# Second MLP: first products as two-by-two blocks with seven products, among the second products

## Chip, cores and metric

The kernel runs on one core of a Trainium2 chip. The metric is the device time of one execution in microseconds. The core has a TensorE (PE, matrix products into PSUM banks), a VectorE (DVE), a ScalarE (ACT), a GpSimd (POOL) and a SyncE (SP) that issues the DMAs between DRAM and SBUF. Each engine runs its own instructions in the order of the program; semaphores tie them together.

## The reference, cut to what matters

Attention with a learnt bias on 4 x 8 heads of 576 tokens gives x of 2304 tokens x 512, then two MLPs follow:

```
x = attn_out ...reshape(2304, 512)
h = x @ w_in           # first MLP: 512 x 2048
g = h - np.tanh(h)
x = g @ w_out          # 2048 x 512
h = x @ w_in           # second MLP, weights of its own
r = np.maximum(h, 0.0)
g = s * (r * r) + b
out = g @ w_out
```

All is float32. The kernel writes each operand as a sum of a rounded part ("hi") and a rest ("lo") in the fp32r format and forms three of the four cross products, so a product costs three matmuls.

## The kernel before, in words

The attention comes first (lines 207 to 555). During it, a part of the first MLP's weights and the first tokens are fetched and split.

Then one loop runs over `seq`, all (c, f): ten chunks c of tokens (five for each MLP: 512 tokens, one chunk of 256 in each) and 16 blocks f of 128 hidden units. Step n does for its (c, f) the **first product** `gemm1` (line 323: 12 matmuls of 128x128 weights by the chunk's columns into one of two PSUM banks `h`), the `gate` (ACT squashes, DVE combines; in the second MLP a DVE scale and shift follows) and, one step later, the `split` (ACT casts to hi, DVE subtracts to lo). Two steps later comes the **second product** `gemm2` (line 567): in the first MLP 12 matmuls with the weights standing, in the second MLP three for each 128 tokens, with the tokens standing and 512 output columns. It adds up over f in PSUM banks `a0` to `a3`, which leave over SBUF to DRAM (`x2_d`, or `out_x`) after the 16th f.

PE's order in a step is thus: first product of n, second product of n-2.

**Weights** arrive as raw 64-bit words (two 32-bit halves; 512 KB for 128x512 numbers). Decoding one is `begin` (POOL takes the sign, ACT scales), `high` and `low` (two DVE instructions), and `both` (ACT casts, POOL subtracts). `weights_tick` does one stage each of three pieces; the step decides by `want` how many are due. In the last chunk of the first MLP the loop fetches the second MLP's pieces (`fetch(16 + m)`, line 618), into the slots of the first, two per step. **Tokens** of the next chunk are loaded and split on the POOL in steps 5 to 14 of a chunk (`load_x`, lines 298 to 319).

All DMAs of the loop are issued by SP in the order of the program, save two of the very end (line 603). `ring` (line 295) is a pool of 11 SBUF tiles of 576 columns.

## Time and profile before

| | us |
|---|---|
| median of 3 runs | 1073.44 (1071.9 to 1073.63) |
| the profiled execution | 1073.4 |
| its span, first to last instruction | 1071.6 |
| PE busy | 1059.9 |
| DVE busy | 575.9 |
| ACT busy | 461.9 |
| POOL busy | 339.3 |

The attention ends at about us 273 of the span, the first MLP runs to about 680, the second to the end. Busy times are shares of the whole span. The granted TensorE clock of the profiled execution was 1.0 throughout. To read a row of a timeline: its start in us, its length in us, engine, line of the kernel, operation, tiles, shape and how many instructions are merged in it. A merged row of matmuls is longer than the distance to the next row, because the modelled end of one overlaps the next; the pace is the distance between starts.

### The profile page before, as it was taken

To read this page: it belongs to the slowest core of one execution; us is meant where nothing else is said; L and a number is where in the kernel's file an instruction comes from. 1 tells how busy PE (TensorE), PEld (TensorE's weight loads), DVE (VectorE), ACT (ScalarE), POOL (GpSimd) and SP (SyncE) were. 2 spreads that over 40 slices of the span, in tenths; PEclk is the share of its full clock that TensorE was granted. 3 is DMA by queue.
4 is the path that set the end of the run, shared out by engine and by line. 5 is a ranking of instruction groups with operands and counts; after the bars stand their busy time and mean duration, and the time that the engine had idled before them with its cause. 6 is when DMAs were issued, how large, how long until landed. Compare 5 with 4: busy or idle time off the path is not lost.

```text
span 1071.6 us, 18296 instructions
## 1 busy us (share of the span) xinstructions
PE 1059.9 (99%) x7000; PEld 836.5 (78%) x7000; DVE 575.9 (54%) x1159; ACT 461.9 (43%) x955; POOL 339.3 (32%) x518
## 2 busy tenths in 40 slices
...
GB/s 285 321 188 262 194 228 155 185 128 89 119 273 20 31 30 1 1 80 20 40 1 1 189 214 205 158 10 10 69 11 1 40 40 1 1 59 1 1 40 20
DMA packets 41335, 99.66 MB, mean 93 GB/s; under 512 B 5024, under 2 KB 11552, under 8 KB 41248
## 3 DMA queue, kind: packets, MB, share of 16 engines
...
q10 hardware_dynamic: 288, 0.26, 0.1%
...
## 4 chain that ended last, share of the span: by engine, by line
PE 90%; DVE 2%; POOL 1%; DMA 1%; issue 1%; ACT 0%; ACTq 0%; DVEq 0%; POOLq 0%
PE h L333 37%; PE a L587 37%; PE o L497 7%; PE s L398 6%; PE t L442 3%; POOL pn L436 1%; DMA qk<-in_qk 1%; PE c L442 1%; DVE raw L405 1%; ACT p L419 0%; DVE xo L504 0%; POOL w L89 0%; DVE pt L480 0%; DVE sm L427 0%; POOL sm L423 0%
## 5 line engine op out<-in xcount | busy, mean ns | idle before, releaser
L333 PE MATMUL h<-x,w 128*128 128x512 f32 (+1 forms) x1920 | 420.6, 368 | 0.0
L333 PEld LDWEIGHTS h<-x,w 128*128 128x128 f32 x1920 | 337.4, 188 | 62.4 <-issue 0.8
L342 DVE TENSOR_TENSOR h<-h,ring 128x512 f32<-128x512 f32 (+1 forms) x160 | 103.4, 646 | 348.2 <-ACT ring L341 348.1
L341 ACT ACTIVATE ring<-h 128x512 f32<-128x512 f32 (+1 forms) x160 | 88.8, 555 | 375.0 <-PE h L333 375.0
L587 PE MATMUL a<-ring,w 128*128 128x512 f32 (+1 forms) x960 | 210.2, 368 | 0.0
L587 PE MATMUL a<-w,ring 128*128 128x512 f32 x864 | 208.9, 389 | 0.0
L587 PEld LDWEIGHTS a<-ring,w 128*128 128x128 f32 x960 | 168.3, 189 | 30.0
L587 PEld LDWEIGHTS a<-w,ring 128*128 128x128 f32 x864 | 161.1, 188 | 32.7
L349 ACT CAST ring<-h 128x512 fp32r<-128x512 f32 (+1 forms) x160 | 87.1, 544 | 142.8 <-DVE h L344 108.0
L436 POOL TENSOR_SCALAR pn<-p,sm 128x576 f32<-128x576 f32 (+2 forms) x224 | 131.8, 605 | 41.5 <-DVE sm L427 37.1
L350 DVE TENSOR_TENSOR ring<-h,ring 128x512 fp32r<-128x512 f32 (+1 forms) x160 | 101.8, 636 | 74.0 <-ACT ring L349 69.2
L86 POOL TENSOR_SCALAR x<-xr 128x512 fp32r<-128x512 f32 (+1 forms) x36 | 20.6, 572 | 339.1 <-DMA xr<-x_d 339.1
L405 DVE CUSTOM_DVE_ANT_0 raw<-s,bias 128x576 f32<-128x576 f32 x144 | 103.8, 753 | 20.3 <-PE s L398 14.9
L419 ACT ACTIVATE p<-raw,mn 128x576 f32<-128x576 f32 x144 | 110.9, 774 | 7.7 <-DVE mn L405 4.3
L89 POOL TENSOR_TENSOR w<-wx,w 128x512 fp32r<-128x512 f32 x64 | 82.8, 1294 | 84.9 <-ACT w L148 82.8
L497 PE MATMUL o<-pt,vv 128*64 128x256 f32 (+1 forms) x640 | 95.0, 418 | 1.3 <-DVE xo L504 1.3
L398 PE MATMUL s<-qk 64*128 64x288 f32 (+1 forms) x640 | 91.7, 430 | 2.7 <-DVE mn L405 1.3
L398 PEld LDWEIGHTS s<-qk 64*128 64x128 f32 (+1 forms) x640 | 46.9, 175 | 43.9 <-DVE mn L405 18.3
L126 POOL TENSOR_SCALAR wsg<-w 128x512 f32<-128x512 f32 x64 | 41.8, 653 | 83.4 <-DMA w<-in_wts 82.8
L344 DVE TENSOR_SCALAR h<-h,sb_t 128x512 f32<-128x512 f32 (+1 forms) x80 | 61.2, 765 | 2.9
L442 PEld LDWEIGHTS t<-ident,pn 64*128 64x128 f32 x1184 | 51.8, 139 | 9.9 <-DVE pt L480 1.5
L497 PEld LDWEIGHTS o<-pt,vv 128*64 128x64 f32 x640 | 38.9, 136 | 24.1 <-DVE xo L504 1.7
...
## 6 DMA issues: line engine op xcount, KB each, us to landing
w<-in_wts SPq DMA_DIRECT2D x64, 512.0 KB, 4.9
...
```

What stands on the lines that cost most here:

```text
L333: nc.tensor.matmul(h, a, x, start=(k == 0), stop=(k == 3 * KD - 1))
L341: nc.scalar.activation(out=t, in_=h, func=(AF.Tanh, AF.Relu)[layer])
L342: nc.vector.tensor_tensor(out=h, in0=h, in1=t, op=(ALU.subtract, ALU.mult)[layer])
L349: nc.scalar.copy(gh, g)
L350: nc.vector.tensor_tensor(out=gl, in0=g, in1=gh.bitcast(F32), op=ALU.subtract)
L398: nc.tensor.matmul(o[0:n, c, 0:288], q[h, ee, t * 128:t * 128 + n], kk[h, ee], start=True, stop=True)
L405: nc.vector.tensor_tensor_reduce(out=raw.rearrange("p (c j) -> p c j", c=2), in0=s_t.pop((x, j))[:, :, 0:288], in1=bias_t[pairs[i][0], k]. ...
L419: nc.scalar.activation(out=p, in_=raw, func=AF.Exp, scale=-1.0, bias=mn, accum_out=sm[:, j:j + 1])
L436: nc.gpsimd.tensor_scalar(out=pn[:, c:c + b - a], in0=p[:, a:b], scalar1=sm[:, j:j + 1], scalar2=0.0, op0=ALU.mult, op1=ALU.add)
L442: nc.tensor.transpose(out_, in_, ident[ROWS[r], ROWS[r]])
L497: nc.tensor.matmul(o[h], v[:, e, j], unit_t[i, u][:, 8 if j == 4 else 4 * e + j, 0:n], start=(j == 0), stop=(j == 4))
L587: nc.tensor.matmul(o, x, y, start=first and j == 0, stop=last and j == 2)
```

## The change

The second MLP no longer runs in the loop over chunks. Its tokens are taken as three blocks of 768 (`SUPER`), each as two halves of 384 columns. For a pair p of hidden blocks (f = 2p and 2p+1) the first product is a two-by-two block product: two halves of the 512 input rows, two hidden blocks, two halves of tokens. It is formed with **seven products** in place of eight: sums of weight blocks times sums of token blocks, and sums of the results in PSUM (`X`, `Y`, `Z`, `V`, lines 833 to 874 of the changed kernel). A product is six matmuls of 384 columns. Two of the pair's four result blocks (first half of the tokens) go on at once, split into g1 and g2, and their second products stand among the next pair's products. The other two are held in SBUF and split later: after eight pairs, the second half's 16 second products run as one stretch, during which the next block's tokens are summed and split.

The second MLP's raw weights are fetched from step 18 of the first MLP on, one piece per step (`raw_next`, `keep`), decoded to float32 and stored to a DRAM tensor `w32_d`. The weights of a pair's first product are read back for each block (`load_w`), summed on the POOL (`combine`) and split on ACT and POOL (`part`). The second products' weights are read back once in the last chunk of the first MLP (`renew`, `renewed`). SBUF pools are arranged anew under one naming function (`place`); in the attention 11 raw loads of single pieces stand where 7 loads of two did.

**PE, second MLP.** Before, two groups of one step (h: first product, a: accumulators of the second; x tokens, w weights, ring the split units):

```order
L333 MATMUL h<-x_9918,w_8133 128x512 x6
L333 MATMUL h<-x_10059,w_8133 128x512 x6
L587 MATMUL a_10274<-w_8087,ring 128x512 x3
L587 MATMUL a_10278<-w_8087,ring 128x512 x3
L587 MATMUL a_10282<-w_8087,ring 128x512 x3
L587 MATMUL a_10286<-w_8087,ring 128x512 x3
```

After, one pair of the last block (XA, C: sums of tokens and of weights, split; a: accumulators of the first half's tokens):

```order
L828 MATMUL X<-XA,C_11015 128x384 x6
L828 MATMUL Y<-C_10725,C_11015 128x384 x6
L828 MATMUL Z<-C_10725,C_11015 128x384 x6
L828 MATMUL V<-XA,C_11015 128x384 x6
L582 MATMUL a_11043<-w_8071,ring 128x512 x3
L582 MATMUL a_11047<-w_8071,ring 128x512 x3
L582 MATMUL a_11051<-w_8071,ring 128x512 x3
L828 MATMUL X<-C_10725,C_11015 128x384 x3
L828 MATMUL X<-C_10806,C_11015 128x384 x3
L828 MATMUL Z<-C_10806,C_11015 128x384 x6
L828 MATMUL V<-C_10806,C_11015 128x384 x6
```

The first products moved from one bank of 512 columns to four banks of 384, with second products of the pair before between them; X, Z and V are each written twice.

**DVE, second MLP.** Before, two steps (multiply, scale and shift, subtract the cast):

```order
L342 TENSOR_TENSOR h_10671<-h_10671,ring_10684 128x512
L344 TENSOR_SCALAR h_10671<-h_10671,sb_t_82 128x512
L350 TENSOR_TENSOR ring_10689<-h_10671,ring_10688 128x512
L342 TENSOR_TENSOR h_10706<-h_10706,ring_10719 128x512
L344 TENSOR_SCALAR h_10706<-h_10706,sb_t_82 128x512
L350 TENSOR_TENSOR ring_10724<-h_10706,ring_10723 128x512
```

After, most of one pair (L844 to L846 sums of results, L734 and L727 multiply, L729 scale and shift, L741 subtract the cast):

```order
L844 TENSOR_TENSOR ring_11671<-Z_11667,ring_11670 128x384
L846 TENSOR_TENSOR Y_11666<-V_11668,ring_11671 128x384
L734 TENSOR_TENSOR Y_11666<-Y_11666,ring_11709 128x384
L727 TENSOR_TENSOR X_11665<-X_11665,ring_11720 128x384
L729 TENSOR_SCALAR X_11665<-X_11665,sb_t_77 128x384
L857 TENSOR_TENSOR Z_11667<-Z_11667,ring_11670 128x384
L741 TENSOR_TENSOR ring_11732<-X_11665,ring_11731 128x384
L727 TENSOR_TENSOR Z_11667<-Z_11667,ring_11735 128x384
L729 TENSOR_SCALAR Z_11667<-Z_11667,sb_t_77 128x384
L863 TENSOR_TENSOR V_11668<-V_11668,ring_11670 128x384
L741 TENSOR_TENSOR ring_11749<-Z_11667,ring_11748 128x384
L734 TENSOR_TENSOR V_11668<-V_11668,ring_11746 128x384
```

The three instructions of a step became thirteen of a pair, and those of X, Z and V follow one another on the four banks.

**SP, the 256-column chunk of the first MLP.** Before, the tokens of two next chunks and the stores of a finished chunk:

```order
L307 DMA xr<-x_d_72 128x256
L307 DMA xr<-x_d_73 128x256
L307 DMA xr<-x_d_74 128x256
L307 DMA xr<-x_d_75 128x256
L593 DMA x_d<-o 128x512 x4
L307 DMA xr<-x_d_72 128x512
L307 DMA xr<-x_d_73 128x512
```

After, the same stretch (st: raw pieces, w_d: the DRAM tensor of decoded weights, s: decoded pieces and tokens):

```order
L612 DMA w_d<-s_6572 128x512
L604 DMA st_6612<-in_wts 128x512
L612 DMA w_d<-s_6614 128x512
L588 DMA x_d<-ring 128x512 x4
L604 DMA st_6666<-in_wts 128x512
L612 DMA w_d<-s_6668 128x512
L604 DMA st_6712<-in_wts 128x512
L612 DMA w_d<-s_6714 128x512
L604 DMA st_6754<-in_wts 128x512
```

Between the token loads and the chunk's stores there now stand a raw load and a store of each step.

The diff, cut to its core:

```diff
-FT = {4 + 6 * F: F for F in range(7)}
+FT = {4 + 4 * k: k for k in range(11)}
...
-CHUNKS += [(1, i * 512, min(512, NT - i * 512)) for i in range(5)]
-NC1 = 5
-XF, XL, FF = 5, 3, 11
+SUPER = [(1, i) for i in range(3)]
+C1 = 18
...
+        def raw_next(j):
+            F, h = wq[j]
+            raw = place(f"st{j % 2}", [512], I64)
+            nc.sync.dma_start(out=raw, in_=wts[16 + F, h])
+            raw_w[32 + j] = words(raw)
+
+        def keep(j):
+            k = 32 + j
+            begin(k, raw_w.pop(k))
+            high(k)
+            low(k)
+            nc.sync.dma_start(out=w32_d[wq[j]], in_=wx_t.pop(k)[1])
...
+        def renew(f):
+            wx_t[f] = ring(F32)[:, 0:512]
+            nc.sync.dma_start(out=wx_t[f], in_=w32_d[f, 1])
+
+        def renewed(f):
+            x = wx_t.pop(f)
+            w = wt[f, 1] = weight(f, 1)
+            nc.scalar.copy(w[:, 0], x)
+            rest(w[:, 1], x, w[:, 0])
...
+        def load_w(q, p):
+            if p >= NF // 2:
+                q, p = q + 1, p - NF // 2
+            if q < len(SUPER):
+                wf_t[q, p] = place(f"st{p % 2}", [2, 512])
+                nc.sync.dma_start(out=wf_t[q, p], in_=w32_d[2 * p:2 * p + 2, 0].rearrange("f p n -> p f n"))
+
+        def combine(q, p):
...
+            w = wf_t[q, p]
+            a11, a12, a21, a22 = (w[:, j // 2, j % 2 * 256:j % 2 * 256 + 256] for j in range(4))
+            sums_ = sums_at[q, p] = place("XB", [4, 256])
+            s2, s3, s1, s4 = (sums_[:, j] for j in range(4))
+            for o, a, b, op in ((s1, a21, a22, ALU.add), (s2, s1, a11, ALU.subtract), (s3, a11, a21, ALU.subtract),
+                                (s4, a12, s2, ALU.subtract)):
+                nc.gpsimd.tensor_tensor(out=o, in0=a, in1=b, op=op)
+
+        def part(q, p):
+            w, sums_ = wf_t.pop((q, p)), sums_at.pop((q, p))
+            cs = cs_t[q, p] = place(f"C{(p + q) % 2}", [7, 2, 256], F32R)
...
+            for o, x in groups:
+                nc.scalar.copy(cs[:, o, 0], x)
+            for o, x in groups:
+                rest(cs[:, o, 1], x, cs[:, o, 0])
...
+            def put(u, i, x):
...
+                nc.scalar.copy(unit(u, i, 0), x)
+                nc.vector.tensor_tensor(out=unit(u, i, 1), in0=x, in1=unit(u, i, 0).bitcast(F32), op=ALU.subtract)
+
+            def minus(o, a, b):
+                nc.vector.tensor_tensor(out=o, in0=a, in1=b, op=ALU.subtract)
+
+            def first(i):
+                put(0, i, raw(i, 0))
+                minus(raw(i, 0), raw(i, 1), raw(i, 0))
+                put(3, i, raw(i, 0))
...
+            return [lambda: load(0, 2), lambda: load(1, 3)] + [lambda g=g, i=i: g(i) for g in (first, second, third, fourth, fifth, sixth)
+                                                              for i in range(2)]
...
+        def squashed(layer, c):
+            t = ring(F32)[:, 0:384]
+            nc.scalar.activation(out=t, in_=c, func=(AF.Tanh, AF.Relu)[layer])
+            return t
+
+        def now_units(layer, c, t):
+            nc.vector.tensor_tensor(out=c, in0=c, in1=t, op=(ALU.subtract, ALU.mult)[layer])
+            if layer:
+                nc.vector.tensor_scalar(out=c, in0=c, scalar1=sb_t[:, 0:1], scalar2=sb_t[:, 1:2], op0=ALU.mult, op1=ALU.add)
...
+        def later_units(layer, c, t, f):
+            g = held_unit(f)
+            if layer:
+                nc.vector.tensor_tensor(out=c, in0=c, in1=t, op=ALU.mult)
+                nc.scalar.activation(out=g, in_=c, func=AF.Identity, scale=sb_t[:, 0:1], bias=sb_t[:, 1:2])
...
+        def parted(x, gs):
+            nc.scalar.copy(gs[0], x)
+            nc.vector.tensor_tensor(out=gs[1], in0=x, in1=gs[0].bitcast(F32), op=ALU.subtract)
...
-            m = n - swap - LAG - 1
-            if 0 <= m < 16:
-                fetch(16 + m)
-            if FF + n < 16:
-                fetch(FF + n)
-            if m >= 1:
-                want = 32 + min(32, int(1.4 * m))
...
+            if C1 <= n < C1 + 32:
+                raw_next(n - C1)
+            if C1 < n <= C1 + 32:
+                keep(n - C1 - 1)
...
+            e = n - (NS - NF)
+            if e == 2:
+                load_w(0, 0)
+                load_w(0, 1)
+            if e == 6:
+                combine(0, 0)
+                part(0, 0)
+                combine(0, 1)
+            for _ in range({8: 2, 10: 1, 11: 1, 12: 2, 13: 2, 14: 2, 15: 1}.get(e, 0)):
+                xq.pop(0)()
+            if SUPER[0][0] and e >= LAG:
+                if e - LAG >= 1:
+                    renewed(e - LAG - 1)
+                renew(e - LAG)
...
+        fill = [lambda: gemm2(*seq[-2]), lambda: gemm2(*seq[-1])]
+        for q, (layer, s_) in enumerate(SUPER):
...
+            def product(o, p, a, u, begins):
+                cs = cs_t[q, p]
+                for i in range(2):
+                    for j, (l, r) in enumerate(((0, 0), (0, 1), (1, 0))):
+                        nc.tensor.matmul(o, cs[:, a, l, i * 128:i * 128 + 128], unit(u, i, r),
+                                         start=begins and i == 0 and j == 0, stop=i == 1 and j == 2,
+                                         skip_group_check=not begins)
+
+            pend = []
+            for p in range(NF // 2):
+                X, Y, Z, V = (bank(t) for t in "XYZV")
+                load_w(q, p + 2)
+                m1, u2, r = (ring(F32)[:, 0:384] for _ in range(3))
+                product(X, p, 4, 0, True)
+                nc.scalar.copy(m1, X)
+                if p + 1 < NF // 2:
+                    part(q, p + 1)
+                product(Y, p, 0, 1, True)
+                nc.vector.tensor_tensor(out=u2, in0=Y, in1=m1, op=ALU.add)
+                product(Z, p, 1, 2, True)
+                nc.vector.tensor_tensor(out=r, in0=Z, in1=u2, op=ALU.add)
+                product(V, p, 2, 3, True)
+                nc.vector.tensor_tensor(out=Y, in0=V, in1=r, op=ALU.add)
+                if pend:
+                    second_products(0, 2 * p - 2, pend.pop(0))
+                elif fill:
+                    fill.pop(0)()
+                t = squashed(layer, Y)
+                later_units(layer, Y, t, 2 * p + 1)
+                product(X, p, 5, 4, False)
+                t = squashed(layer, X)
+                now_units(layer, X, t)
+                product(Z, p, 6, 5, False)
+                nc.vector.tensor_tensor(out=Z, in0=Z, in1=u2, op=ALU.add)
+                g1 = two()
+                parted(X, g1)
+                t = squashed(layer, Z)
+                now_units(layer, Z, t)
+                product(V, p, 3, 6, False)
+                nc.vector.tensor_tensor(out=V, in0=V, in1=u2, op=ALU.add)
+                t = squashed(layer, V)
+                g2 = two()
+                parted(Z, g2)
+                later_units(layer, V, t, 2 * p)
+                if pend:
+                    second_products(0, 2 * p - 1, pend.pop(0))
+                elif fill:
+                    fill.pop(0)()
+                pend = [g1, g2]
+                if p + 1 < NF // 2:
+                    combine(q, p + 2)
...
+            xq = [] if final else tokens(q + 1)
+            for _ in range(2):
+                if xq:
+                    xq.pop(0)()
+            gs = {}
+
+            def ahead(f):
+                gs[f] = two()
+                parted(held_unit(f), gs[f])
+
+            ahead(0)
+            second_products(0, NF - 2, pend.pop(0))
+            ahead(1)
+            second_products(0, NF - 1, pend.pop(0))
+            if not final:
+                part(q + 1, 0)
+                combine(q + 1, 1)
+            for f in range(NF):
+                if f + 2 < NF:
+                    ahead(f + 2)
+                if f >= 2 and xq:
+                    xq.pop(0)()
+                if f >= 0:
+                    second_products(1, f, gs.pop(f))
+            while xq:
+                xq.pop(0)()
```

## Rows read from the trace of the kernel before

**Rows 1.** Page, part 1: engine, busy us (share of the span), instructions.

```profile
PE 1059.9 (99%) x7000; PEld 836.5 (78%) x7000; DVE 575.9 (54%) x1159; ACT 461.9 (43%) x955; POOL 339.3 (32%) x518
```

**Rows 2.** Timeline of PE in us 495 to 513: start, length, engine, line, operation, tiles, count.

```profile
495.95 1.60 PE L587 MATMUL a<-ring,w 128*128 128x256 f32 x12
497.39 2.91 PE L333 MATMUL h<-x,w 128*128 128x512 f32 x12
500.14 1.60 PE L587 MATMUL a<-ring,w 128*128 128x256 f32 x12
501.57 2.91 PE L333 MATMUL h<-x,w 128*128 128x512 f32 x12
...
508.50 2.88 PE L587 MATMUL a<-ring,w 128*128 128x512 f32 x12
511.22 2.88 PE L333 MATMUL h<-x,w 128*128 128x512 f32 x12
```

**Rows 3.** Groups by shape, whole span: line, engine, operation, shapes, count | busy us, mean ns | idle before.

```profile
L333 PEld LDWEIGHTS h<-x,w 128*128 128x128 f32 x1920 | 337.4, 188 | 62.4 <-issue 0.8 <-DVE ring L350 0.5
...
L342 DVE TENSOR_TENSOR h<-h,ring 128x512 f32<-128x512 f32 x128 | 89.5, 700 | 308.1 <-ACT ring L341 308.0
...
L89 POOL TENSOR_TENSOR w<-wx,w 128x512 fp32r<-128x512 f32 x64 | 82.8, 1294 | 84.9 <-ACT w L148 82.8 <-DVE sm L427 1.5 <-DMA w<-in_wts 0.3
...
L341 ACT ACTIVATE ring<-h 128x512 f32<-128x512 f32 x128 | 76.5, 598 | 330.7 <-PE h L333 330.7
L349 ACT CAST ring<-h 128x512 fp32r<-128x512 f32 x128 | 75.2, 587 | 118.2 <-DVE h L344 90.9 <-DVE h L342 27.3
...
L344 DVE TENSOR_SCALAR h<-h,sb_t 128x512 f32<-128x512 f32 x64 | 52.4, 819 | 2.3
...
L342 DVE TENSOR_TENSOR h<-h,ring 128x256 f32<-128x256 f32 x32 | 13.8, 432 | 40.1 <-ACT ring L341 40.1
...
L341 ACT ACTIVATE ring<-h 128x256 f32<-128x256 f32 x32 | 12.3, 384 | 44.4 <-PE h L333 44.4
...
L344 DVE TENSOR_SCALAR h<-h,sb_t 128x256 f32<-128x256 f32 x16 | 8.8, 551 | 0.6
...
L89 POOL TENSOR_TENSOR x<-xr,x 128x256 fp32r<-128x256 f32 x8 | 5.9, 738 | 0.7
```

**Rows 4.** Timeline of all engines over one step of the second MLP.

```profile
960.02 2.88 PE L587 MATMUL a<-w,ring 128*128 128x512 f32 x12
...
960.22 0.60 ACT L341 ACTIVATE ring<-h 128x512 f32<-128x512 f32 x1 [2.58 <-PE h L333]
960.85 0.70 DVE L342 TENSOR_TENSOR h<-h,ring 128x512 f32<-128x512 f32 x1 [2.49 <-ACT ring L341]
961.58 0.82 DVE L344 TENSOR_SCALAR h<-h,sb_t 128x512 f32<-128x512 f32 x1
962.49 0.58 ACT L349 CAST ring<-h 128x512 fp32r<-128x512 f32 x1 [1.68 <-DVE h L344]
```

**Rows 5.** Timeline of ACT and DVE in us 625 to 631.

```profile
625.70 0.62 ACT L148 CAST w<-wx 128x512 fp32r<-128x512 f32 x1 [0.61 <-DVE wx L140]
...
626.22 0.63 ACT L127 ACTIVATE y<-w 128x512 f32<-128x512 f32 x1
...
629.01 0.70 DVE L342 TENSOR_TENSOR h<-h,ring 128x512 f32<-128x512 f32 x1 [1.49 <-ACT ring L341]
...
629.61 0.69 DVE L133 SCALAR_TENSOR_TENSOR y<-y,wsg 128x512 int32<-128x512 int32 x1
```

**Rows 6.** SP's timeline at 642.8, then DMA issues of two stretches: count, KB, median us to landing.

```profile
642.82 0.42 SPq L113 DMA_DIRECT2D w<-in_wts  x1
...
w<-in_wts SPq DMA_DIRECT2D x1, 512.0 KB, 3.5
...
w<-in_wts SPq DMA_DIRECT2D x21, 512.0 KB, 4.3
```

**Rows 7.** Instructions of line 133 in the attention: ns min/median/max, first and last start.

```profile
L133 DVE SCALAR_TENSOR_TENSOR wx<-wx,wsg x8: 670/678/1790, 93.8 to 255.2; 128x512 int32<-128x512 int32 x8
```

281 lines of the change are left out of this document (178 added, 103 removed).

## The prediction

> **What bounds the kernel now.** I read the page's busy times first: the TensorE (PE) is busy for 99% of the span, the DVE (VectorE) for 54%, the ACT (ScalarE) for 43%, the POOL (GpSimd) for 32% [rows 1]. The PE is the bound, so any product that is saved is worth its full pace, as long as nothing new makes the PE wait. Next the timeline of the PE: in both MLPs groups of twelve products follow one another without a gap. A group of 512 columns starts 2.72 us before the next one, a group of 256 columns 1.44 us; where the two sizes alternate, a couple takes 2.75 + 1.43 = 4.18 us in place of 4.16 [rows 2]. So one product takes 226.7 ns at 512 columns and 120 ns at 256: 32 columns' worth beyond its own columns at 2.4 columns per ns, and 173.3 ns at 384 (an estimate on the line through the two rows).
>
> Then the work beside it: the groups by shape give the durations of the vector work at 512 and 256 columns, from which I take 384 halfway [rows 3]: relu 0.49 us (ACT), product or sum of a PSUM tile and an SBUF tile 0.57 (DVE), scale and shift 0.69 (DVE), cast 0.48 (ACT), and the subtraction of the cast like the product, 0.56 (DVE). One step's timeline gives the joints: a product's result is taken up 0.20 us after the next group starts, ACT to DVE and a DVE instruction that needs the one before cost 0.03, DVE to ACT 0.09 [rows 4]. Instructions of one engine that don't need each other overlap by 0.10 [rows 5].
>
> **The first products of the second MLP.** Before: four chunks of 16 groups at 2.72 and one of 16 at 1.44, 174.1 + 23.0 = 197.1 us [rows 2]. After: 3 blocks of 768 tokens x 8 pairs x 7 products x 6 matmuls = 1008 matmuls of 384 columns, 174.7 us. **Saved: 22.4 us.** The second products stay as they are (864 matmuls of 512 columns). The 384- and 512-column groups now alternate some 45 times at 0.02 each: **+0.9**.
>
> **The wait inside a pair.** A pair's PE work is X, Y, Z, V (4.16 us), nine second products (2.04), X, Z, V again (3.12), nine more (2.04): 11.36 us. Four PSUM banks serve it, so pair p+1 can't start Z before the split of Z of pair p has read it, nor V before the scale and shift of V has. I follow the chain from the end of X's last product (0): relu X 0.20 to 0.69, multiply 1.29, scale and shift 2.00, Z + u2 1.91 to 2.48 (overlapped), cast X 2.09 to 2.57, subtraction 3.17, relu Z to 3.06, multiply 3.10 to 3.66, scale and shift 4.38, V + u2 to 4.86, relu V 4.95 to 5.44, cast Z to 5.82, subtraction 6.42; then multiply V 6.89, scale and shift on the ACT 7.46. The PE, without waits, wants Z again at 2.08 + 2.04 + 2.08 = 6.20 and V at 7.24. With 0.1 for taking up a release it waits some 0.3 for each, of which V's wait holds Z's: 0.37 us per pair. It is the same in the next pair, since the DVE and the ACT then wait for X again. It bites from pair 1 to pair 7, six times a block, 18 times: **+6.7**. Bounds: 0 (chain 0.4 shorter) and 16 (0.9 each, 0.04 more on each of 15 instructions).
>
> **Pair 0 of the second and third block** has no second products to put between. The V sum ends at 4.93, relu and multiply of Y at 6.11, the ACT's scale and shift of Y at 6.68, and relu X, behind it on the ACT, starts at 6.58, 1.18 us later than its data. So X is free only at 9.55 where the PE wants it at 7.28 (2.4 lost), and Z at 12.80 where it then wants it at 11.73 (1.2): 3.55 each, **+7.1** for two; bounds 5 and 9. In the first block's pair 0 the last two steps of the first MLP fill the gaps with 2.72 each: nothing.
>
> **Raw weights beside the first MLP.** From step 18 on, each step loads one raw piece (512 KB), decodes it (ACT 0.63, DVE twice 0.69 [rows 5]) and stores it. In steps of 5.44 us this has room. In the 256-column chunk a step has 2.88 us. There are two staging tiles, so the load for step n+2 goes out after the decode of n and after its store on SP: 0.06 + 0.42 for the issue [rows 6], then the landing, 0.06, then 0.63 + 0.04 + 0.69 + 0.04 + 0.69. Two steps thus take 2.63 us + landing, and 5.76 are there: it closes at 3.1 us. In the trace such a load, 512 KB at the head of a burst, lands in 3.5 us; the median of its stage, where two or three go out together, is 4.3 [rows 6]. I take 3.8, since one store of half the size is ahead of it: 0.67 late per two steps. The ACT runs the decode ahead of the tanh of the step, so the lateness goes into the tanh, the split, and the two h banks; the PE feels it after about 2.2 us (3.5 us from the decode's start to the bank's release, against 5.76). The load of step 34 also stands behind the four stores of the finished chunk, which wait for the last accumulator's copy: about 2.7 late at once. 2.7 + 5 x 0.67 - 2.2 = **+3.9**; bounds 0 (landing 3.1) and 7 (landing 4.3).
> What the Trainium skill says here, page "DMA: Bandwidth & Descriptors", section "Anatomy of one DMA": about 2.0 us fixed plus the bytes at 436 GB/s, fitted on another path than SP's; that gives an estimate of 3.2 us, no trace row shows less than 3.5, and by it this term would be under 1 us.
>
> **Second halves.** While the PE runs 16 x 2.04 us of second products, the DVE subtracts held units from their casts, both operands in SBUF. In the first 7 us the POOL splits the next block's first weights. Of 8 DVE instructions with two SBUF operands in the attention, most took 0.67 us and the longest 1.79 [rows 7]: it stood behind a POOL instruction. The longest POOL instruction here has 1024 elements, 2.4 us (1.29 at 512, 0.74 at 256 [rows 3]). The subtraction for the third f is due 1.3 us after its cast. I take 0.5 in each of two blocks, **+1.0**; bounds 0 and 4.8.
>
> **At nothing.** Per pair the DVE has 13 instructions (7.6 us), the ACT 12 (6.4 with the weight parts), the POOL four sums and three splits (7.4), all under 11.36; their order is what costs, above. The weight loads (512 KB per pair) are issued a pair ahead. The 16 reloads of second weights stand a step ahead of their use in steps of 5.44 us; without that cover the ACT would wait in order, ahead of the split, some 2 us. The token sums have 12 steps of 2.04. In the attention 11 loads stand where 14 did: nothing, within 1 us. The tail has one more pair of stores, issued while products still run.
>
> **Sum** against the profiled execution (1073.4 us; span 1071.6, 1.8 around it; the median of the three runs is 1073.44, the same): -22.4 + 0.9 + 6.7 + 7.1 + 3.9 + 1.0 = -2.8, so 1070.6 us. A measurement of this kernel can tell about 0.2%, 2.1 us: it is a gain that is hardly larger.
>
> **Rivals.** *The chains close.* If the raw loads land in 3.1 us or the steps before them leave more room, and the pair's chain is 0.4 shorter, only pair 0 remains: -22.4 + 0.9 + 7.1 = -14.4, 1059.0; with one of the two open up to 1066. For it: DMA engines and vector engines are far from busy on the mean. Against: no row shows 3.1.
> *The pair's chain is longer* (the one that ends slower). Place: the split of Z, which ends the DVE's part of each pair. If each of its 15 instructions takes 0.04 more than halfway between the rows, a pair waits 0.97 and 18 of them 17.5: 1081.4. It is slower than before from 0.53 us per pair on. For it: four banks without a spare, and two engines in strict turns. Against: the same instructions kept 0.70 and 0.69 also while other engines were busy [rows 5].
> *The POOL holds the second halves.* Each of two blocks loses 2.4 us at its third f, +4.8 in place of 1.0: 1074.4. It holds if a subtraction waits for the whole POOL instruction, as the 1.79 us hint [rows 7]. The Trainium skill, page "SBUF — State Buffer", section "Who interferes with whom", says so: a DVE instruction with two SBUF inputs and a GpSimd one that reads SBUF exclude each other for the whole instruction. By that rule the pair's own chain is free, as each of its instructions has one PSUM operand.
> *The saving isn't there.* If 384 columns were paced by the weight load (188 ns [rows 3]), 1008 matmuls would take 14.8 us more: 1085.4. Against: 256 columns run at 120 ns [rows 2].
>
> **How the numbers follow.** Forecast 0.41 (1066 to 1076; about half of it, 0.22, under 1071.3, 0.16 within 0.2%, 0.03 above 1075.6). Chains close 0.25. Longer chain 0.24. POOL 0.08, within 0.2%. Weight pace 0.02. Faster 0.22 + 0.25 = 0.47; same 0.16 + 0.08 = 0.24; slower 0.03 + 0.24 + 0.02 = 0.29. The range 1059 to 1081 holds the forecast, the POOL case, most of the closing chains and half of the longer chain: a little over 0.8.
>
> **What would show it.** Groups of six 384-column products 1.04 us apart; PE waits on the DVE and ACT of some 0.4 us before Z and V in 18 pairs, and of 2.4 and 1.2 us at the second pair of the last two blocks; in the 256-column chunk ACT waits on raw loads and PE waits on the h banks that grow from the middle of the chunk; waits at the third f of a second half. Wrong it is if the PE waits elsewhere, above all at the start of the first block (a unit or a weight part that is late), or if the landings differ from 3.8 us.

## The result, and the profile after

The changed kernel takes **1082.1 us** (median of 4 runs, 1082.07 to 1082.66) where the kernel before took 1073.0 beside it: a ratio of **1.0087**, 95% interval 1.007 to 1.0105. It is slower by 0.9%, 9 us. The forecast was 1070.6 with a range of 1059 to 1081, so the time lies above the range and on the other side of no change.

The page's busy times, part 1 (engine, busy us, share of the span, instructions), under the span; to be read against [rows 1]:

```profile
span 1080.3 us, 19163 instructions
...
PE 1056.2 (98%) x7048; PEld 841.4 (78%) x7048; DVE 652.5 (60%) x1345; ACT 557.0 (52%) x1158; POOL 460.6 (43%) x630
```

PE's busy time fell by only 3.7 us, though 22.4 us of products went (in the last kernel below, which has the same products, it is 1040.3): a part of PE's lateness stands in its busy time. So I take the stages apart by the starts of groups on PE. PE's timeline, of before and then of after, where the first MLP begins and where the second one does (start, length, line, tiles, count):

```profile
273.70 3.02 PE L333 MATMUL h<-x,w 128*128 128x512 f32 x12
...
668.98 2.88 PE L333 MATMUL h<-x,w 128*128 128x512 f32 x12
```

```profile
272.56 3.02 PE L340 MATMUL h<-X,C 128*128 128x512 f32 x12
...
674.35 1.23 PE L828 MATMUL X<-XA,C 128*128 128x384 f32 x6
```

The attention ends 1.1 us earlier, yet the second MLP begins 5.4 us later: the first MLP lost **6.5 us**. From its first product to the end of the span the second MLP takes 406.0 us (1080.3 - 674.35) where it took 402.6: **3.3 more**, with 22.4 us of products saved. Both stages of the forecast came out worse.

Two pairs of the last blocks, on PE. The first fence is pair 5 of the second block, where everything is in its steady state; the second is the change from pair 0 to pair 1, also of the second block (in brackets: idle before, and who ended it):

```profile
870.42 1.23 PE L828 MATMUL X<-XA,C 128*128 128x384 f32 x6
871.49 1.21 PE L828 MATMUL Y<-C,C 128*128 128x384 f32 x6
872.64 1.34 PE L828 MATMUL Z<-C,C 128*128 128x384 f32 x6
873.82 1.32 PE L828 MATMUL V<-XA,C 128*128 128x384 f32 x6
874.99 2.25 PE L582 MATMUL a<-w,ring 128*128 128x512 f32 x9
877.08 1.23 PE L828 MATMUL X<-C,C 128*128 128x384 f32 x6
878.14 1.20 PE L828 MATMUL Z<-C,C 128*128 128x384 f32 x6
...
882.30 1.23 PE L828 MATMUL X<-XA,C 128*128 128x384 f32 x6
```

```profile
812.30 1.23 PE L828 MATMUL X<-XA,C 128*128 128x384 f32 x6
...
821.94 1.33 PE L828 MATMUL X<-XA,C 128*128 128x384 f32 x6 [2.17 <-DVE ring L741]
...
825.10 1.32 PE L828 MATMUL Z<-C,C 128*128 128x384 f32 x6 [0.78 <-DVE ring L741]
...
834.74 1.23 PE L828 MATMUL X<-XA,C 128*128 128x384 f32 x6
```

A steady pair takes 11.88 us (882.30 - 870.42). Groups that wait for nothing stand 1.04 to 1.07 apart, as forecast from [rows 2]; Z comes 1.15 after Y and V 1.18 after Z, and the second products 1.17 after V. A pair without any wait takes 11.49 (it is seen below); so a steady pair waits 0.38. Pairs 0 and 1 of the second block take 22.44 together, where 7.30 and 11.49 would do: 3.65 of waits.

The stages of all kernels that were run. "Start" is the first product of the second MLP; "pairs 1 to 3" are of the first block; "0 + 1" are the first two pairs of the second and of the third block; "pair 7 + half" reaches from the start of pair 7 to the next block's start, of the first and of the second block. All but "start" are differences of group starts on PE, in us; the ratio is to the kernel before, run beside it each time (medians from 1072.1 to 1073.0).

| kernel | start | steady pair | pairs 1 to 3 | 0 + 1 | pair 7 + half | span | median | ratio (95%) |
|---|---|---|---|---|---|---|---|---|
| before | 668.98 | | | | | 1071.6 | 1073.0 | 1 |
| after | 674.35 | 11.87 | 38.14 | 22.44, 22.46 | 51.26, 51.21 | 1080.3 | 1082.1 | 1.0087 (1.007 to 1.0105) |
| e_raw | 666.83 | 11.87 | 38.13 | 22.44, 22.44 | 51.21, 51.20 | 1073.0 | 1075.6 | 1.0029 (1.0018 to 1.0039) |
| e_noload | 667.60 | 11.88 | 38.13 | 22.44, 22.46 | 51.24, 51.24 | 1073.7 | 1075.8 | 1.0036 (1.0023 to 1.0049) |
| e_renew | 674.87 | 11.86 | 35.43 | 22.46, 22.44 | 51.21, 51.23 | 1078.2 | 1080.3 | 1.0071 (1.0056 to 1.0086) |
| e_swap | 674.81 | 11.49 | 35.66 | 22.71, 21.68 | 50.64, 50.64 | 1071.6 | 1074.0 | 1.0013 (1.0003 to 1.0023) |
| e_toks | 674.23 | 11.88 | 37.98 | 22.76, 23.11 | 49.35, 49.38 | 1077.3 | 1079.1 | 1.0060 (1.0045 to 1.0075) |
| e_fill | 674.38 | 11.88 | 38.14 | 23.38, 23.35 | 47.15, 47.13 | 1074.3 | 1075.7 | 1.0033 (1.0020 to 1.0046) |
| c_four | 667.19 | 11.49 | 34.48 | 21.66, 22.77 | 48.72, 48.76 | 1059.0 | 1062.1 | 0.9902 (0.9888 to 0.9917) |
| c_lock | 668.10 | 11.49 | 34.48 | 21.67, 22.81 | 48.21, 48.21 | 1058.8 | 1060.3 | 0.9888 (0.9872 to 0.9905) |
| c_fill | 668.44 | 11.49 | 34.48 | 22.99, 22.99 | 44.13, 44.13 | 1052.3 | 1053.8 | 0.9824 (0.9811 to 0.9838) |
| e_wait | 675.41 | 11.88 | 38.13 | 25.72, 25.75 | 51.24, 51.27 | 1088.0 | 1089.1 | 1.0157 (1.0139 to 1.0176) |

Read the row "after" against the ideal: three slow pairs in the first block (38.14, where three steady ones are 35.6), 3.65 us twice in "0 + 1", and a second half of 51.2 where 48.21 is possible. Four places, then, and the first MLP's 256-column chunk ahead of them. The experiments take them one by one.

### The profile page after: what moved, and what is told of

Same layout as the page of the kernel before. It is cut to its first block, busy times and chain, and to the rows that moved or that the text cites. A ratio compares the mean times of both kernels' runs of the same rounds, so it can differ in the third digit from the quotient of the medians.

```text
span 1080.3 us, 19163 instructions
## 1 busy us (share of the span) xinstructions
PE 1056.2 (98%) x7048; PEld 841.4 (78%) x7048; DVE 652.5 (60%) x1345; ACT 557.0 (52%) x1158; POOL 460.6 (43%) x630
## 4 chain that ended last, share of the span: by engine, by line
PE 77%; DVE 6%; POOL 4%; issue 3%; ACT 3%; DMA 2%; SPq 0%; ACTq 0%; POOLq 0%; DVEq 0%
PE a L582 25%; PE h L340 17%; PE o L504 7%; PE s L405 6%; PE Z L828 4%; PE V L828 4%; PE X L828 4%; PE t L449 3%; PE Z L582 3%; PE V L582 2%; DMA st<-in_wts 2%; PE Y L828 2%; POOL C L92 1%; POOL pn L443 1%; DVE ring L741 1%
## 5 line engine op out<-in xcount | busy, mean ns | idle before, releaser
L582 PE MATMUL a<-w,ring 128*128 128x512 f32 x576 | 147.0, 392 | 0.0
L349 DVE TENSOR_TENSOR h<-h,ring 128x512 f32<-128x512 f32 (+1 forms) x80 | 51.6, 645 | 143.8 <-ACT ring L348 143.7
L348 ACT ACTIVATE ring<-h 128x512 f32<-128x512 f32 (+1 forms) x80 | 44.2, 553 | 165.5 <-PE h L340 165.5
L582 PEld LDWEIGHTS a<-w,ring 128*128 128x128 f32 x576 | 107.6, 188 | 20.8
L340 PE MATMUL h<-X,C 128*128 128x512 f32 (+1 forms) x576 | 119.2, 356 | 3.9 <-DVE ring L357 3.8
L92 POOL TENSOR_TENSOR C<-st,C 128x512 fp32r<-128x512 f32 (+1 forms) x48 | 48.0, 1023 | 166.5 <-ACT C L652 166.5
L412 DVE CUSTOM_DVE_ANT_0 raw<-s,bias 128x576 f32<-128x576 f32 x144 | 103.9, 753 | 19.6 <-PE s L405 14.0
L340 PEld LDWEIGHTS h<-X,C 128*128 128x128 f32 x576 | 96.0, 189 | 22.0 <-DVE ring L357 6.2
L357 DVE TENSOR_TENSOR ring<-h,ring 128x512 fp32r<-128x512 f32 (+1 forms) x80 | 50.9, 637 | 38.2 <-ACT ring L356 38.2
L340 PE MATMUL h<-XA,C 128*128 128x512 f32 x288 | 70.7, 390 | 0.0
L828 PE MATMUL Z<-C,C 128*128 128x384 f32 x288 | 60.3, 344 | 3.0 <-DVE ring L741 3.0
L340 PEld LDWEIGHTS h<-XA,C 128*128 128x128 f32 x288 | 53.8, 188 | 11.3 <-issue 0.2
```

Source lines behind the costliest of these rows:

```text
L92: nc.gpsimd.tensor_tensor(out=lo, in0=raw, in1=hi.bitcast(F32), op=ALU.subtract)
L340: nc.tensor.matmul(h, a, x, start=(k == 0), stop=(k == 3 * KD - 1))
L348: nc.scalar.activation(out=t, in_=h, func=(AF.Tanh, AF.Relu)[layer])
L349: nc.vector.tensor_tensor(out=h, in0=h, in1=t, op=(ALU.subtract, ALU.mult)[layer])
L357: nc.vector.tensor_tensor(out=gl, in0=g, in1=gh.bitcast(F32), op=ALU.subtract)
L412: nc.vector.tensor_tensor_reduce(out=raw.rearrange("p (c j) -> p c j", c=2), in0=s_t.pop((x, j))[:, :, 0:288], in1=bias_t[pairs[i][0], k]. ...
```

## Experiment 1: raw pieces out of the 256-column chunk

```diff
+        RAW_AT = [*range(18, 32), *range(48, 66)]
-            if C1 <= n < C1 + 32:
-                raw_next(n - C1)
-            if C1 < n <= C1 + 32:
-                keep(n - C1 - 1)
+            if n in RAW_AT:
+                raw_next(RAW_AT.index(n))
+            if n - 1 in RAW_AT:
+                keep(RAW_AT.index(n - 1))
```

> The changed kernel, but no raw weight piece is loaded, decoded or stored in the 256-column chunk of the first MLP: pieces 0 to 13 stay at steps 18 to 31, the other 18 move to steps 48 to 65. In the changed kernel the first product of the second MLP starts at us 674.35 of the span, 5.4 later than before although the attention ended 1.1 earlier. Theory (the loads and decodes don't fit into steps of 2.88 us): some 6.5 us come back, the first product of the second MLP starts at about 667.9, total about 1075.6. Rival (a step of 5.44 us next to the last chunk's token loads is full as well, the lateness only moves): it starts between 672 and 674, total 1080 to 1082.

Measured: start 666.83, 7.5 us earlier than in the changed kernel, total 1075.6. Of the 7.5, 1.0 stands ahead of the first MLP, which starts at 271.56 in place of 272.56; the first MLP itself takes 395.27, as before (395.28), in place of 401.79. All later stages are the same to 0.1 us, so the 6.5 us are back: the loss was in this chunk, and steps of 5.44 us have room for the same work.

## Experiment 2: the decodes without the loads

```diff
-            raw = place(f"st{j % 2}", [512], I64)
-            nc.sync.dma_start(out=raw, in_=wts[16 + F, h])
-            raw_w[32 + j] = words(raw)
+            if not 14 <= j < 30:
+                staged[j % 2] = place(f"st{j % 2}", [512], I64)
+                nc.sync.dma_start(out=staged[j % 2], in_=wts[16 + F, h])
+            raw_w[32 + j] = words(staged[j % 2])
```

> The changed kernel without the 16 raw loads of the 256-column chunk: the pieces of steps 32 to 47 are decoded and stored as ever, but from the two staging tiles as they were filled before, so these weights are wrong and the time is read alone. Theory (a load's landing of 3.7 us in a loop of two staging tiles sets these steps): the steps take 2.9 us, the first product of the second MLP starts at about 668 in place of 674.35, total about 1075.6. Rival (the ACT and the DVE in turns set them: cast 0.37, scale 0.66, two decoding steps 1.39, the gate's subtraction 0.42 and the joints are 3.0 us without any landing): of 6.5 us at least 1.5 stay if it is that alone, nearly all if the DVE's place in the order is what counts; 670 to 674, total 1077 to 1082.

Measured: start 667.60, total 1075.8; so without the raw loads nothing of the loss is left, and decode and gate fit. The ACT's timeline of one step here (L137: decode; L348: gate):

```profile
484.40 0.66 ACT L137 ACTIVATE y<-st 128x512 f32<-128x512 f32 x1
...
486.13 0.38 ACT L348 ACTIVATE ring<-h 128x256 f32<-128x256 f32 x1 [1.07 <-PE h L340]
...
487.28 0.66 ACT L137 ACTIVATE y<-st 128x512 f32<-128x512 f32 x1
```

L137 recurs after 2.88 us, and the gate waits for PE (1.07): PE leads. In the changed kernel the same stretch reads, with SP's issues (L604 load, L612 store, L314 token load):

```profile
484.15 0.58 SPq L314 DMA_DIRECT2D s<-x_d  x1
...
484.84 0.39 SPq L604 DMA_DIRECT2D st<-in_wts  x1
...
484.97 0.63 ACT L137 ACTIVATE y<-st 128x512 f32<-128x512 f32 x1 [0.52 <-DMA st<-in_wts]
...
487.22 0.32 SPq L612 DMA_DIRECT2D w_d<-s  x1
...
487.71 0.33 SPq L604 DMA_DIRECT2D st<-in_wts  x1
...
488.56 0.64 ACT L137 ACTIVATE y<-st 128x512 f32<-128x512 f32 x1 [0.63 <-DMA st<-in_wts]
...
492.03 0.63 ACT L137 ACTIVATE y<-st 128x512 f32<-128x512 f32 x1 [0.49 <-DMA st<-in_wts]
```

This is the forecast's loop of two steps with its real numbers: decode 2.25 (484.97 to 487.22; the sign from the POOL is 0.1 later than the scaling on the ACT), store ahead of the load 0.49, from the load's issue to its use 4.32. Sum 7.06 where 5.76 are there: 1.3 late per two steps. The forecast had 2.63 + 3.8 = 6.43, 0.67 late. The load of the step before has the same sum in other parts: SP issues a token load between the store (483.73) and it, so it goes out 1.11 behind the store and is used 3.72 later (484.84 to 488.56); with a decode of 2.25 that is 7.08. From 470 to 495 the two kinds alternate, with 6.9 to 7.5 us for two steps. In this chunk such a load lands in 3.9 us (median of 14), between the 3.5 and 4.3 of [rows 6]:

```profile
st<-in_wts SPq DMA_DIRECT2D x14, 512.0 KB, 3.9
```

The Trainium skill, page "DMA: Bandwidth & Descriptors", section "Anatomy of one DMA", would give an estimate of 3.2 us for these bytes, by a line fitted on another path than SP's; the measured 3.9 decides, and by it this term is not small.

## Experiment 3: the three late rereads

```diff
-                renew(e - LAG)
+                if e - LAG < NF - 3:
+                    renew(e - LAG)
...
+                again = NF - 6 + p if q == 0 and p in (3, 4, 5) else None
+                if again is not None:
+                    renew(again)
...
                 t = squashed(layer, Z)
+                if again is not None:
+                    renewed(again)
                 now_units(layer, Z, t)
...
-                if q == 0 and p == 0 and layer:
-                    renewed(NF - 3)
-                    for f in (NF - 2, NF - 1):
-                        renew(f)
-                if q == 0 and p == 1 and layer:
-                    for f in (NF - 2, NF - 1):
-                        renewed(f)
```

> The changed kernel, but the last three second weights of the second MLP are read back and split in pairs 3, 4 and 5 of the first block (cast on the ACT behind the relu of Z, where the ACT waits 1.8 us for the DVE) in place of pairs 0 and 1. In the changed kernel pairs 1, 2 and 3 of the first block take 12.78, 12.85 and 12.51 us, a later pair 11.87. Theory (these three casts, and the tile that one of them holds until the POOL has subtracted, delay the copy of X and with it the chain of the pair): pairs 2 and 3 fall to about 11.9, pair 1 to 12.3, total 1082.1 - 2.0 = about 1080. Rival (the first pairs are slow because of the copies of the first MLP's last accumulators alone): pair times stay within 0.2, total within 1 us of 1082.1.

Measured: pairs 1 to 3 take 35.43 in place of 38.14 (11.49, 12.05 and 11.89 each), 2.7 less, so the place is right. The total, 1080.3, is 1.8 less; in this execution the first MLP took 0.9 more. How it came about shows in the changed kernel, where pair 0 of the first block ends and pair 1 begins:

```profile
691.48 1.30 POOL L92 TENSOR_TENSOR w<-ring,w 128x512 fp32r<-128x512 f32 x1 [5.72 <-ACT w L621]
...
692.81 0.48 ACT L838 COPY ring<-X 128x384 f32<-128x384 f32 x1 [1.41 <-POOL w L92]
...
699.98 1.34 PE L828 MATMUL X<-XA,C 128*128 128x384 f32 x6 [0.86 <-DVE ring L741]
```

L621 is the cast of a reread weight, L838 the ACT's copy of X. The copy needs a ring tile, and in the order of the program the one that comes up still holds the reread weights. It waits 1.41 us until the POOL has subtracted them, and everything of the pair stands behind that copy. PE pays 0.86 a pair later.

## Experiment 4: the cast of Z ahead of the relu of V

```diff
-                t = squashed(layer, V)
                 g2 = two()
                 parted(Z, g2)
+                t = squashed(layer, V)
                 later_units(layer, V, t, 2 * p)
```

> The changed kernel with one thing in another order: the cast of Z stands ahead of the relu of V on the ACT, not behind it. In the changed kernel a pair takes 11.87 us where its products without a wait take 11.49. Theory (the forecast's chain through the DVE and the ACT sets Z's and V's release): Z comes free 0.77 us and V 0.63 us earlier, both waits go, a pair takes 11.5, and 18 pairs give 6.9 us, the first block's early pairs a little more: about 1074.5. Rival (a wait is left in any case, since the PE's group after it starts slowly, or the four banks have no spare): a pair stays above 11.75, total 1080 or more.

Measured: a steady pair takes **11.49**, total 1074.0. One changed place in the ACT's order is worth 8.1 us. 2.5 of them stand in pairs 1 to 3 of the first block (35.66 for 38.14), where a steady wait of 0.38 would account for 1.1. The end of the chain of pair 4, second block, in the changed kernel (L729 scale and shift of Z, L723 relu of V, L740 and L741 split of Z):

```profile
869.96 0.68 DVE L729 TENSOR_SCALAR Z<-Z,sb_t 128x384 f32<-128x384 f32 x1
...
871.14 0.49 ACT L723 ACTIVATE ring<-V 128x384 f32<-128x384 f32 x1 [1.82 <-DVE V L863]
...
871.53 0.47 ACT L740 CAST ring<-Z 128x384 fp32r<-128x384 f32 x1
872.03 0.56 DVE L741 TENSOR_TENSOR ring<-Z,ring 128x384 fp32r<-128x384 f32 x1 [0.93 <-ACT ring L740]
```

And in the kernel with the other order:

```profile
876.67 0.68 DVE L729 TENSOR_SCALAR Z<-Z,sb_t 128x384 f32<-128x384 f32 x1
...
877.39 0.48 ACT L740 CAST ring<-Z 128x384 fp32r<-128x384 f32 x1 [1.35 <-DVE Z L729]
877.85 0.49 ACT L723 ACTIVATE ring<-V 128x384 f32<-128x384 f32 x1
877.90 0.56 DVE L741 TENSOR_TENSOR ring<-Z,ring 128x384 fp32r<-128x384 f32 x1
```

From the scale and shift of Z to the end of its split it is 2.63 us (869.96 to 872.59) in the one and 1.79 (876.67 to 878.46) in the other. In the changed kernel Z is free at 872.59 and PE takes it at 872.64; V is free after its scale and shift, at 873.77, and PE takes it at 873.82. The chain sets both, as the forecast worked out, and nothing else is left of the wait when it is shorter.

## Experiment 5: token subtractions one step ahead

```diff
             def first(i):
                 put(0, i, raw(i, 0))
+
+            def first_sum(i):
                 minus(raw(i, 0), raw(i, 1), raw(i, 0))
+
+            def first_rest(i):
                 put(3, i, raw(i, 0))
 
             def second(i):
+                put(1, i, raw(i, 0))
+
+            def second_sum(i):
                 minus(raw(i, 0), raw(2 + i, 1), raw(i, 0))
-                put(1, i, raw(i, 0))
...
+                    steps((first, 0), (first_sum, 0)), steps((first_rest, 0), (first, 1), (first_sum, 1), (second_sum, 0)),
+                    steps((first_rest, 1), (second_sum, 1)), steps((second, 0), (third_sum, 0)), steps((second, 1), (third_sum, 1)),
```

> The changed kernel, but each subtraction that forms a token sum for the next block stands one step ahead of its cast, so that the ACT's cast no longer waits for a DVE instruction that stands behind another cast's subtraction. In the changed kernel the second halves of the first two blocks take 35.3 us for 32.6 us of products. Theory (ACT and DVE in strict turns need 2.1 to 2.6 us for a step of 2.04): some 2.0 of the 2.6 us of each half go, 0.5 at the third and fourth hidden block stays with the POOL; total 1082.1 - 4 = about 1078. Rival (DVE instructions with two SBUF operands are held up by the POOL, all of the 2.6): the halves stay at 35 us, total 1081 to 1082.

Measured: pair 7 and half take 49.35 and 49.38 (51.26 and 51.21), total 1079.1. The 1.9 us per half are as expected; 1.0 us is given back in "0 + 1", where the granted clock fell (last section). The turns in the changed kernel, one hidden block of the second half (L681, L682: cast and rest of a token sum; L740, L741: of a held unit; L685: subtraction that forms the next sum):

```profile
791.54 0.51 ACT L681 CAST C<-C 128x384 fp32r<-128x384 f32 x1 [1.15 <-DVE C L685]
...
791.96 0.51 ACT L740 CAST ring<-X 128x384 fp32r<-128x384 f32 x1
792.09 0.56 DVE L682 TENSOR_TENSOR C<-C,C 128x384 fp32r<-128x384 f32 x1 [0.58 <-ACT C L681]
792.56 0.55 DVE L741 TENSOR_TENSOR ring<-X,ring 128x384 fp32r<-128x384 f32 x1
...
793.03 0.55 DVE L685 TENSOR_TENSOR C<-C 128x384 f32<-128x384 f32 x1
...
793.62 0.51 ACT L681 CAST C<-C 128x384 fp32r<-128x384 f32 x1 [1.15 <-DVE C L685]
```

Neither engine is full: the DVE is busy for 1.5 us of 2.08 and the ACT for 0.9. But the ACT waits 1.15 for L685, which stands last on the DVE, and the DVE then waits 0.58 for the ACT. A round takes 2.08 with one subtraction and 2.54 with two (793.62 to 796.16), where PE needs a unit every 2.04.

## Experiment 6: cover for pair 0

```diff
-            def second_products(half, f, gs):
-                order = (["a0", "a1", "a2", "a3"], ["V", "Y", "Z", "X"] if not layer else ["Z", "V", "a3"])[half][:nd]
+            def second_products(half, f, gs, accs=accs, c0=c0, nd=nd, cols=cols, final=final, layer=layer):
+                order = (["a0", "a1", "a2", "a3"], ["V", "Y", "Z", "X"] if not layer else ["a3", "a0", "a1"])[half][:nd]
...
-                if f >= 0:
+                if f < NF - 2 or final:
                     second_products(1, f, gs.pop(f))
+                else:
+                    fill.append(lambda run=second_products, f=f, g=gs.pop(f): run(1, f, g))
```

> The changed kernel, but the last two hidden blocks of a second half (not of the last block) run among the products of pair 0 of the next block, and the second half's accumulators are a3, a0 and a1 in place of Z, V and a3. In the changed kernel pairs 0 and 1 of the second and third block take 9.64 and 12.80 us, with waits of 2.2 us at X and 0.8 at Z. Theory (pair 0 lacks cover): pair 0 takes 11.5 with its 4.2 of second products, without a wait, pair 1 about 12.3, since three copies now stand ahead of it as in the first block; 2 x (9.64 + 4.1 + 12.80 - 11.5 - 12.3) = 5.4 less, total about 1076.7. Rival (the copies of the accumulators then stand in pair 0's chain and take back what the cover gave): pair 1 above 13.5, total 1080 to 1083.

Measured: pair 0 takes 11.49 and pair 1 11.89 and 11.86; with 4.1 us less in each half, total 1075.7. Pair 1 is even a steady one: the three copies cost nothing that shows.

## Experiments 7 and 8: four edits together, and the POOL out of the way

> The four edits tried one by one so far (raw pieces out of the 256-column chunk, three reread weights in pairs 3 to 5, the cast of Z ahead of the relu of V, token subtractions one step ahead) in one kernel. Theory (they touch four separate stages): the gains add up, 6.6 + 1.9 + 8.1 + 3.0 = 19.6 less, somewhat under that since the second and third act on the same pairs: 1062 to 1064. Rival (an engine becomes the bound, or waits move into one another): above 1066.

Measured: 1062.1, 20.0 us below the changed kernel; the single gains were 6.6, 1.8, 8.1 and 3.0, sum 19.6. The totals add up within their spread (the ten executions of e_swap alone lie between 1071.3 and 1075.4). By stages one place is shared: pairs 1 to 3 of the first block gain 2.7 by the moved rereads alone and 2.5 by the swap alone, but 3.7 by both (38.14 to 34.48), not 5.2. With a shorter chain of the pair most of the late rereads no longer reaches PE; the other losses lie apart.

The eighth kernel adds to it:

```diff
-        def part(q, p):
+        def part(q, p, engine=nc.gpsimd):
...
-                rest(cs[:, o, 1], x, cs[:, o, 0])
+                engine.tensor_tensor(out=cs[:, o, 1], in0=x, in1=cs[:, o, 0].bitcast(F32), op=ALU.subtract)
...
-            if not final:
-                part(q + 1, 0)
-                combine(q + 1, 1)
...
+                if f == 1 and not final:
+                    part(q + 1, 0, nc.vector)
+                if f == 10 and not final:
+                    combine(q + 1, 1)
```

> As the kernel with the four edits, and in the second halves the POOL has nothing to do while the DVE subtracts casts: the rests of the next block's first weights are formed by the DVE, and the sums of its second weights stand at hidden block 10. Theory (a DVE instruction with two SBUF operands waits for a POOL instruction that runs): the three DVE subtractions that took 4.46 us beside the POOL's 2.7 take 0.56 each, a second half falls from 33.4 to about 32.8, total 1.2 less than with the four edits. Rival (those 4.46 us are the DVE waiting for its own operands): the subtractions stay above 1 us, the total is the same or higher by the DVE's 2.2 us of extra work.

Measured: pair 7 and half fall from 48.74 to 48.21, which is 11.49 for the pair, two times 2.04 and 16 times 2.04: no wait is left. The total falls by 1.8, more than the 1.0 of the two halves, but the executions of the two kernels overlap, so it is the halves that show the effect. What the POOL did in the changed kernel, and then the three subtractions beside it (count, ns min/median/max, first and last start; 4.47 us together):

```profile
780.61 2.71 POOL L92 TENSOR_TENSOR C<-XB,C 128x1024 fp32r<-128x1024 f32 x1
```

```profile
L741 DVE TENSOR_TENSOR ring<-X,ring x3: 791/1082/2747, 780.3 to 783.7; 128x384 fp32r<-128x384 f32 x3
```

One of the three took 2.75 us in place of 0.56, beside a POOL instruction of 2.71: the same sight as the 1.79 us of [rows 7] (at 231.71, beside a POOL subtraction of 1.27 at 231.67). In the eighth kernel, in the first of these stretches:

```profile
770.27 0.98 POOL L644 TENSOR_TENSOR XB<-st 128x256 f32<-128x256 f32 x1 [20.89 <-DVE C L654]
...
772.61 1.09 DVE L754 TENSOR_TENSOR ring<-X,ring 128x384 fp32r<-128x384 f32 x1
```

The longest subtraction of a cast is 1.09, beside a POOL sum of 256 elements (772.24). So this kernel does less than was meant: the sums stand at hidden block 10 in the program, but the POOL has nothing ahead of them and runs them as soon as the DVE has read the old ones, from 770.27 on, at hidden blocks 2 to 4. What went is the POOL's long subtractions, and what is left beside the sums costs PE nothing. Instructions of the pairs that read PSUM are not held up. In the changed kernel, a sum of two results while the POOL subtracts (two POOL instructions in one row):

```profile
874.74 2.01 POOL L92 TENSOR_TENSOR C<-st,C 128x512 fp32r<-128x512 f32 x2 [4.47 <-ACT C L652]
...
875.50 0.57 DVE L846 TENSOR_TENSOR Y<-V,ring 128x384 f32<-128x384 f32 x1
```

It takes the 0.57 us that such a sum was forecast to take.

That is what the Trainium skill states, page "SBUF — State Buffer", section "Who interferes with whom": a DVE instruction with two SBUF inputs and a GpSimd one that reads SBUF exclude each other. The trace agrees, for the one that is held and for those that are not, and the run gives the price here: 0.5 us for PE in each half.

## Experiment 9: everything together

> The kernel with the four edits and the POOL's work moved out of the second halves (1060.3 us), and in addition the last two hidden blocks of a second half among the products of the next block's pair 0. There pairs 0 and 1 of the last two blocks took 9.65 + 12.02 and 9.65 + 13.16 us; the 13.16 had some 2 us at a granted clock of 0.5 after PE's wait of 2.2 us. Theory (the cover is enough and the chain closes; without a wait of this length the clock stays at 1.0): both pairs take 11.5, 4.1 us of which leave the second halves; 2.8 + 3.9 = 6.7 less, about 1053.6, mean clock 1.0. Rival (three copies of accumulators stand in a chain without slack): pair 1 above 12.5, total 1055.5 or more.

Measured: **1053.8**, ratio 0.9824 (0.9811 to 0.9838): 1.8% faster than the kernel before, and 28 us faster than the changed one with the same arithmetic. PE from pair 0 to pair 2 of the second block:

```profile
794.38 1.23 PE L843 MATMUL X<-XA,C 128*128 128x384 f32 x6
...
798.57 2.24 PE L582 MATMUL a<-w,ring 128*128 128x512 f32 x9
...
805.88 1.23 PE L843 MATMUL X<-XA,C 128*128 128x384 f32 x6
...
817.37 1.23 PE L843 MATMUL X<-XA,C 128*128 128x384 f32 x6
```

No group waits; a pair is 11.49 to 11.50 throughout (but for pair 0 of the first block, 12.85 with the first MLP's last second products), and this is the pair without waits that the other kernels are measured by.

## Why the prediction was wrong, step by step

Two steps that the prediction put "At nothing" failed: the token sums in the second halves (+4.3) and the late rereads of weights (+3.0). Two terms were mis-sized: the raw weights (+6.5 for +3.9) and the joints (+2.7 for +0.9).

| term | forecast | measured | by |
|---|---|---|---|
| first products | -22.4 | -22.4 | groups of six 1.04 apart |
| joints between 384 and 512 columns | +0.9 | +2.7 | 21 pairs of 11.49 for 11.36 |
| wait inside a pair | +6.7 | +6.8 | 18 x 0.38, gone in e_swap |
| pairs 1 to 3 of the first block | 0 | +3.0 | 2.7 gone in e_renew, 2.5 in e_swap |
| pair 0 of the last two blocks | +7.1 | +7.3 | 6.4 gone in e_fill |
| raw weights in the 256-column chunk | +3.9 | +6.5 | gone in e_raw and e_noload |
| second halves, POOL | +1.0 | +1.0 | gone in c_lock |
| second halves, ACT and DVE in turns | 0 | +4.3 | 3.7 gone in e_toks |
| attention | 0 | -1.1 | start of the first MLP; within its spread |
| sum | -2.8 | +8.1 | the spans differ by 8.7 |

How the new numbers are worked out: pairs 1 to 6 of the first block take 73.84 (687.20 to 761.04), pair 7 waits 0.38; against 6 x 11.49 and the six waits of 0.38 that the forecast counts for this block that is 3.0 too much. Second halves: 51.26 - 48.21 - 0.38 = 2.67 and 2.62, of which c_lock gives back 0.5 each. After e_fill pair 1 still has the wait of a steady pair. The start of the first MLP lies between 271.56 and 273.12 in the eleven kernels with the same new attention, so the -1.1 is not told from a change between executions. 0.6 us of the 8.7 are not assigned.

- **The saving, right.** 1008 products at 173 ns; the rival that 384 columns are paced by the weight load falls. The joints were mis-sized: in c_fill nine second products ahead of X take 2.08 to the next start in place of 2.04, and X 1.06 to 1.07 in place of 1.04; twice a pair that is 0.13, where the forecast carried 0.02 for some 45 couples. What makes it was not tried.
- **The pair's chain, right** in mechanism and near in size: 0.37 forecast, 0.38 measured. PE takes Z 6.4 us and V 7.6 after X's last product (878.14 to 884.52 and 885.70), forecast 6.42 and 7.46 with 0.1 for taking up. The terms as written give 0.32 (6.42 + 0.1 - 6.20, after which V is free in time), and the wait falls otherwise than forecast: 0.11 ahead of Z, 0.14 ahead of V and 0.13 ahead of the group behind V. That 0.37 and 0.38 agree so closely is in part luck. The same holds for pair 0 (3.55 forecast, 3.65 measured).
- **The rival of a longer chain came nearest in time, by accident.** It gave 1081.4 with 0.97 per pair; the pair waited 0.38. The time was made elsewhere.
- **Raw weights, a mis-sized term.** The loop was right, its sizes were not: in every other step 4.3 to 4.5 us from issue to use in place of 3.8, in most of the steps between 3.7 to 3.8 but the issue 0.4 to 0.6 later behind a token load, which the forecast left out of SP's order; and 0.1 more for the POOL's sign. With 1.3 us late in place of 0.67 the forecast's own sum gives 2.7 + 5 x 1.3 - 2.2 = 7.0. Measured are 6.5 here and 6.9 to 7.6 in the five other kernels that keep this chunk, so the upper bound of 7 came nearer than the forecast. (The least landing in the kernel before is 3.4, twice, not 3.5; none lands in 3.1.) Why a load lands in 3.7 us at one place and in 4.3 at another was not tried.
- **"At nothing", wrong for the token sums.** The step was "The token sums have 12 steps of 2.04". It counted room on each engine and did not follow the order on both: a round through ACT and DVE takes 2.08 to 2.54, and PE lost 2.1 us in each of two halves. I had traced the chain of the pair and not that of the second half.
- **"At nothing", wrong for the rereads.** The prediction looked at the 13 of them that stand in steps of 5.44 us; the last three stand in pairs 0 and 1 of the first block, where a step has no slack, and one of them holds a ring tile. PE lost 3.0 us by it, and that the pair's chain had no slack was part of it (e_swap). "In the first block's pair 0 the last two steps fill the gaps: nothing" was right for pair 0 itself (12.85, without a wait).
- **POOL's hold, right** as to what is held, and for PE 0.5 per half as taken; the rival's 2.4 per block did not come; that the two units split ahead covered the rest is argued from their order.

The forecast's sign hung on 2.8 us out of sums of 20 on either side. Two terms at nothing (7.3 us) and two mis-sized ones (4.4) turned it.

## What to carry to other kernels

A saving on the bound engine is only worth what the order of the others lets through: here 22 us of products came out as a loss of 9, and six edits of order and place turned it into a gain of 19 with the same arithmetic. For each stretch that is moved, write down one round of the turns between two in-order engines, in their real order, and compare its length with the period of the bound engine; busy shares say nothing on it (1.5 of 2.08 us busy, and late). Count the waits on tiles of a shared ring among the turns.

## What the chip showed besides

TensorE's granted clock fell after PE's waits of 2.2 us at pair 1 of the last two blocks, and not each time: at 5 of 16 such places in the eight kernels that have them (none in the changed kernel, in e_raw, e_noload and e_renew; one in e_swap, c_four and c_lock; both in e_toks). There it stood at 0.5, that is 1.2 GHz, for some 3 us, and the two pairs took 0.3 to 1.1 us longer. One kernel made the wait longer:

```diff
+                for _ in range(4 if q and p == 0 else 0):
+                    nc.scalar.copy(m1, m1)
                 t = squashed(layer, X)
```

> The changed kernel with four copies of an SBUF tile onto itself on the ACT ahead of the relu of X in pair 0 of the second and third block, so that PE's wait at X of pair 1 grows from 2.2 to about 4 us. It is to tell what the clock does after such a wait: with 2.2 us it stayed at 1.0 at some of these places and fell to 0.5 at others. Theory (the length of the wait counts): both places show a stretch at 0.5 behind the wait, pairs 0 and 1 together take 1.8 us more for the wait and 1 to 2 more for the clock, total about 1088. Rival (something else than the wait sets it): 1.0 at both places, total about 1085.7.

Measured: 1089.1. With a wait of 4.2 us the clock fell at both places. By stretch, second block (stretch, length, busy time of PE, PEld, DVE, ACT, POOL with counts, granted clock, DMA share, GB/s), and PE's groups behind the wait:

```profile
823.00:824.00 1.00, 0.00 (x0) 0.00 (x0) 0.96 (x3) 0.11 (x1) 0.00 (x1) 0.76 0.00 0
824.00:830.00 6.00, 4.99 (x16) 4.99 (x17) 3.85 (x8) 3.08 (x7) 0.00 (x0) 0.50 0.00 0
```

```profile
825.01 2.29 PE L828 MATMUL X<-XA,C 128*128 128x384 f32 x6 [4.21 <-DVE ring L741]
827.10 2.12 PE L828 MATMUL Y<-C,C 128*128 128x384 f32 x6
```

The clock fell during the wait and stayed at 0.5 for more than 6 us; X's group takes 2.09 to the next, in place of 1.16 at this place in the changed kernel. Pairs 0 and 1 take 3.3 us more than in the changed kernel, 2.0 of them the wait and 1.2 the clock. So a wait of the bound engine can cost more than its length, here 1.2 us behind 4.2, and cover for it (experiment 9) is then worth more than the row of the wait says. Why the 2.2 us waits brought it in some places and not in others, these runs don't tell.
